# A fixed tile plan replaced by a list scheduler with a clock per engine, in a kernel of two attentions whose exponentials run on two engines

## The chip, the cores and the metric

The kernel runs on one core of a Trainium2 chip. The metric is the device time of one execution in microseconds, from the first to the last instruction of the core. Every execution is either "fast" or "slow": slow means over 1.5% above the fastest of the same kernel. Medians are over all executions of a kernel, slow ones too. Profiles are of one execution each.

Engines: TensorE (PE) multiplies, ScalarE (ACT) computes exponentials, VectorE (DVE) does elementwise work and empties PSUM, GpSimd (POOL) masks. Each has its own stream of instructions and waits at semaphores.

## The reference, cut to what matters

Two attention layers with 2048 tokens, 32 heads of 16 channels, each with its projections:

```python
# A: four segments of 512 tokens; causal softmax inside a segment, plus a memory term from earlier segments
logits = einsum('bhqd,bhkd->bhqk', qs, ks) * scale + mask
p = softmax(logits); a_dot = einsum('bhqk,bhkd->bhqd', p, vs)
...                                   # o = g * a_mem + (1 - g) * a_dot; M and z grow by phi(k) v
# B: full softmax attention over 2048 keys
p = softmax(einsum('bhqd,bhkd->bhqk', q, k) * Dh ** -0.5)
o = einsum('bhqk,bhkd->bhqd', p, v)
return concatenate([a, b], -1)        # each after its output projection
```

The work that counts is the exponentials. I call 128 keys by 512 queries of one head a *bank* (one PSUM bank). Four heads are done side by side; four banks with the same keys are a *key block*. Attention B has 512 blocks and A has 80, so there are 592 blocks or 2368 banks. A *unit* is four heads with 512 queries; B has 32 units of 16 blocks.

## The kernel before: the parts that matter

A block's exponentials are computed in one of two ways. On ScalarE: scores in PSUM tiles of three and two banks in turn, one ACTIVATE for a tile. On VectorE: four evacuations write each score, scaled and shifted, as an integer whose bits are an fp16 number (this makes a piecewise linear 2^x), and further passes add other offsets to the integers. The sum over several shifted *patterns*, each multiplied by V into the same accumulator, smooths the error. Every pattern costs four matmuls, and every pattern after the first a pass on VectorE. Lines left out below are marked; options that are switched off are dropped without a mark.

```python
LADDER = (12521, 12721, 12834, 13081, 13329)   # offsets of five patterns
PESHARE = 0.74;  VQUADS = (3, 3);  BANKS = (3, 2);  LAG = 2;  PBUFS = 6;  VBUFS = 9
# ... cut ...
def idle_work(us):            # zeros: matmuls that add nothing, to keep TensorE active
    work[0] = min(max(work[0] - us * PESHARE, -1.0), 0.25)
    acc = accs.get(cur[0])
    while acc is not None and work[0] < -0.11:
        mm(acc[:], zeros[:, 0:P], zeros[:], start=False, stop=False)
# ... cut: all tiles of ScalarE are listed beforehand; VQUADS blocks of every unit of B go to VectorE ...
def vexp(q, buf, x):          # one further pattern
    for i, off in enumerate(LADDER[1:]):
        yield 0.70
        f = vtile()
        nc.vector.tensor_scalar(f[:], x[:], float(off - LADDER[0]), 32767.0, ALU.add, ALU.min)
        vready(q, [1], f); vdone(buf)
def force():
    if pv(NT, 1): return
    if vwork and vlive[0] < VBUFS: vpiece(vwork); return
    assert step_chore()
# ... cut ...
for t in range(NT):           # one tile after the other; times only in units of tiles
    run_until(t)
    scores(t)                 # matmuls of tile t and its exponential; force() if its buffer is not free
    did = pv(t - LAG, 2)      # P x V of up to two blocks of two tiles ago
    # ... cut: one to four pieces of projections, by due tile ...
    idle_work(0.1 + 0.427 * len(tiles[t]))
    flush()
    vfill((0.08 + 0.427 * len(tiles[t])) * VSHARE - 0.69 * vscores(t))
```

## Time and profile before

| | before |
|---|---|
| time, median of four | 1014.6 us (1005.7 to 1027.6; two fast, two slow) |
| the profiled execution | 1026.1 us, slow, mean granted clock 0.955 |
| ScalarE busy / idle | 934.4 / 91.7 us |
| VectorE busy | 726.6 us |
| key blocks on VectorE | 93 (3 for each of 31 units) |

The page's table of busy time (us, share of the span, instructions), and three rows of its 40 slices; a digit is tenths, and PEclk is the clock that TensorE was granted:

```profile
PE 923.2 (90%) x7597; PEld 254.6 (25%) x7721; DVE 726.6 (71%) x1232; ACT 934.4 (91%) x828; POOL 162.2 (16%) x335
...
PE   7898989999898998989899889999989899999986
...
ACT  3799976789999999999999979999999999999984
...
PEclk8999975689999999999999999999999999999988
```

ScalarE is busiest, but in slices 6 to 9 it falls to between 6 and 8 tenths, and the clock to between 5 and 8. TensorE's row stays at 8 and 9 there. So a high busy share of TensorE is not evidence of useful speed. The Trainium skill ("Trainium Kernel Development and Optimization", Performance Expectations) calls matmul busy time a bad metric for how close a kernel is to roofline (the limit of the hardware), because matmuls are pipelined; here it also counts zeros and half-speed work.

The groups of instructions (count | busy us, mean ns of one | idle time just before them and what ended it):

```profile
L648 ACT ACTIVATE pT<-s_ps 128x1536 bf16<-128x1536 f32 (+1 forms) x799 | 923.9, 1313 | 78.1 <-PE s_ps L83 65.1
L685 DVE TENSOR_SCALAR vx<-v_ps 128x512 uint16<-128x512 f32 x372 | 254.1, 684 | 176.5 <-PE s_ps L83 117.9
L608 DVE TENSOR_SCALAR vx<-vx 128x2048 uint16<-128x2048 uint16 x372 | 243.8, 692 | 1.2
...
L83 PE MATMUL acc<-zeros 128*128 128x512 bf16 x401 | 132.4, 398 | 6.9 <-issue 6.8
```

The exponentials cost 923.9 us for (592 - 93) x 4 = 1996 banks: 0.463 us a bank, 1.85 us a block. A pattern pass over 2048 columns (692 ns) costs as much as the evacuation of a single bank of 512 (684 ns). The Trainium skill ("VectorE: DVE Perf Modes", Side-by-side: where the cycles go for N=2048 bf16) gives about 693 ns for 2048 bf16 elements in its fastest mode; these passes over 2048 16-bit integers agree.

Three stretches of the span, and after them one place closer (columns: stretch, length, busy us and count of each engine, granted clock, DMA share, GB/s):

```profile
0.00:50.00 50.00, 40.02 (x259) 13.04 (x264) 21.95 (x39) 27.04 (x25) 28.38 (x70) 0.93 0.73 148
50.00:850.00 800.00, 728.14 (x6060) 200.19 (x6158) 590.56 (x1004) 748.81 (x664) 133.78 (x265) 0.96 0.03 9
850.00:1026.10 176.10, 155.07 (x1283) 41.42 (x1299) 114.05 (x191) 158.51 (x141) 0.00 (x0) 0.95 0.02 7
```

```profile
137.00:216.00 79.00, 71.94 (x438) 14.67 (x445) 45.87 (x80) 55.80 (x49) 9.70 (x19) 0.63 0.01 2
```

ScalarE is the fourth engine column. Between 50 and 850 us it loses 51 us of 800, and 23 of these lie in the 79 us where the clock is 0.63.

### The profile page before, as it was taken

The numbers are of one execution on the slowest core, as the hardware profiler recorded it, in microseconds if no ns is written. First come the engines' busy times: TensorE is split into PE (matmuls) and PEld (weight loads), VectorE is DVE, ScalarE is ACT, GpSimd is POOL, SyncE is SP. The second block draws the span as 40 slices with busy tenths as digits, with TensorE's granted clock in tenths as the row PEclk, the third lists the DMA queues.
The fourth block names the chain that finished last, engine by engine and source line by source line (L and its number), as shares of the span: only waits on it lengthen the run. The fifth ranks groups of instructions, "written<-read, shape, count | busy, mean of one in ns | idle before, by whom it ended". The sixth has DMA issues, their size and how long they took to land.

```text
span 1026.1 us, 18868 instructions
## 1 busy us (share of the span) xinstructions
PE 923.2 (90%) x7597; PEld 254.6 (25%) x7721; DVE 726.6 (71%) x1232; ACT 934.4 (91%) x828; POOL 162.2 (16%) x335
## 2 busy tenths in 40 slices
PE   7898989999898998989899889999989899999986
PEld 2222221122222222222222222222222222222221
DVE  2657665577786888779595868868687698676762
ACT  3799976789999999999999979999999999999984
POOL 3731120030303103040200402003030300000000
PEclk8999975689999999999999999999999999999988
DMA  8500000000001000000001000000000000000000
GB/s 181 107 5 22 1 7 0 7 1 2 6 1 27 22 17 12 1 7 1 6 1 24 14 20 18 6 1 2 6 2 2 1 27 16 1 2 1 1 1 25
DMA packets 35649, 15.47 MB, mean 15 GB/s; under 512 B 27360, under 2 KB 35552, under 8 KB 35552
## 3 DMA queue, kind: packets, MB, share of 16 engines
q1 hardware_dynamic: 33776, 13.78, 5.9%
q8 instruction: 62, 1.02, 0.4%
q10 hardware_dynamic: 1776, 0.40, 0.2%
q14 instruction: 35, 0.29, 0.1%
HBM read 4.20 MB, written 4.19 MB: 8 GB/s over the span
## 4 chain that ended last, share of the span: by engine, by line
ACT 42%; PE 32%; issue 12%; DVE 9%; POOL 2%; DMA 1%; SPq 0%; ACTq 0%; DVEq 0%
ACT pT L648 41%; PE acc L83 14%; PE s_ps L83 8%; PE v_ps L83 6%; DVE vx L685 3%; PE k_ps L83 2%; PE q_ps L83 1%; DVE vx L608 1%; PE o_ps L83 1%; DVE tT L256 1%; ACT ex L197 1%; POOL pT L656 1%; DMA w_a<-in_A_wv_dram 1%; DVE qc L186 1%; SPq L159 0%
## 5 line engine op out<-in xcount | busy, mean ns | idle before, releaser
L648 ACT ACTIVATE pT<-s_ps 128x1536 bf16<-128x1536 f32 (+1 forms) x799 | 923.9, 1313 | 78.1 <-PE s_ps L83 65.1
L685 DVE TENSOR_SCALAR vx<-v_ps 128x512 uint16<-128x512 f32 x372 | 254.1, 684 | 176.5 <-PE s_ps L83 117.9
L83 PE MATMUL s_ps<-qB,KB 32*128 32x512 bf16 x1676 | 319.7, 394 | 33.3 <-ACT pT L648 24.9
L608 DVE TENSOR_SCALAR vx<-vx 128x2048 uint16<-128x2048 uint16 x372 | 243.8, 692 | 1.2
L83 PEld LDWEIGHTS <-KB 32*128 32x128 bf16 x2048 | 94.4, 91 | 322.3 <-issue 313.0
L83 PE MATMUL acc<-vx,VB 128*32 128x512 f16 x1860 | 170.4, 396 | 4.1 <-DVE vx L685 1.7
L83 PE MATMUL v_ps<-qB,KB 32*128 32x512 bf16 x372 | 146.9, 395 | 19.2 <-issue 5.6
L656 POOL TENSOR_SCALAR_AFFINE_SELECT pT<-pT 128x256 bf16<-128x256 bf16 (+2 forms) x242 | 106.1, 466 | 311.8 <-ACT pT L648 310.4
L83 PE MATMUL acc<-pT,VB 128*32 128x512 bf16 x1676 | 155.3, 398 | 0.0
L83 PE MATMUL acc<-zeros 128*128 128x512 bf16 x401 | 132.4, 398 | 6.9 <-issue 6.8
L83 PEld LDWEIGHTS <-VB 128*32 128x32 bf16 x3536 | 56.8, 95 | 141.6 <-issue 140.9
L256 DVE STREAM_TRANSPOSE tT<-acc 128x512 f32<-128x512 f32 x64 | 45.3, 708 | 30.9 <-PE acc L83 30.0
L83 PE MATMUL s_ps<-qA,kA 32*128 32x384 bf16 (+3 forms) x512 | 58.2, 305 | 9.5 <-ACT pT L648 7.1
L83 PEld LDWEIGHTS <-zeros 128*128 128x128 bf16 x480 | 38.8, 99 | 90.5 <-issue 78.3
L189 POOL TENSOR_SCALAR qA<-qc,par 128x512 bf16<-128x512 bf16 x32 | 25.8, 819 | 189.5 <-DVE qc L186 189.4
L189 POOL TENSOR_SCALAR qB<-qc,par 128x512 bf16<-128x512 bf16 x32 | 23.3, 740 | 157.9 <-DVE qc L186 157.9
L83 PE MATMUL acc<-pT,vA 128*32 128x128 bf16 (+3 forms) x512 | 34.9, 313 | 5.7 <-POOL pT L656 3.4
L186 DVE CAST qc<-q_ps 128x512 bf16<-128x512 f32 x32 | 21.9, 683 | 16.2 <-PE q_ps L83 14.6
L83 PEld LDWEIGHTS <-kA 32*128 32x128 bf16 x512 | 17.3, 92 | 50.7 <-issue 46.9
L322 DVE CAST osb<-o_ps 128x512 bf16<-128x512 f32 x28 | 19.2, 684 | 7.7 <-PE o_ps L83 7.3
L83 PE MATMUL v_ps<-w_a,xT_a 128*128 128x512 bf16 x60 | 21.1, 426 | 3.1 <-DMA w_a<-in_A_wv_dram 1.6
L83 PE MATMUL k_ps<-xT_a,w_a 128*128 128x512 bf16 x59 | 20.7, 392 | 2.2 <-DMA xT_a<-in_A_x_dram 1.1
(84 smaller groups left out, 409.7 us busy)
## 6 DMA issues: line engine op xcount, KB each, us to landing
out_dram<-osb SPq DMA_DIRECT2D x31, 128.0 KB, 1.7
w_b<-in_B_wqkv_dram SPq DMA_DIRECT2D x3, 512.0 KB, 5.7
phk<-phkT SPq DMA_TRANSPOSE x48, 2.3
w_a<-in_A_wv_dram SPq DMA_DIRECT2D x1, 512.0 KB, 7.2
wo_a<-in_A_wo_dram SPq DMA_DIRECT2D x1, 512.0 KB, 4.4
wo_b<-in_B_wo_dram SPq DMA_DIRECT2D x1, 512.0 KB, 5.2
w_a<-in_A_wk_dram SPq DMA_DIRECT2D x1, 384.0 KB, 8.8
w_a<-in_A_wq_dram SPq DMA_DIRECT2D x1, 384.0 KB, 9.4
```

The costliest lines, as they stand in the source:

```text
L83: return pin(nc.tensor.matmul(out, lhsT, rhs, **k))
L186: vlater(0.69, lambda: pin(nc.vector.tensor_copy(qc[:], ps[:])))
L189: pin(nc.gpsimd.tensor_scalar(dst[:, e, :], qc[:], par[:, e:e + 1], 0.0, ALU.mult, ALU.add))
L197: pin(nc.scalar.activation(ex[:], src, ACT.Exp))
L256: vlater(0.72, lambda: pin(nc.vector.transpose(st["tT"][:, e].rearrange("p c d -> p (c d)"), acc)))
L322: vlater(0.69, lambda: pin(nc.vector.tensor_copy(osb[:], ps[:])))
L608: pin(nc.vector.tensor_scalar(f[:], x[:], float(off - LADDER[0]), 32767.0, ALU.add, ALU.min))
L648: pin(nc.scalar.activation(pT[:, 0:n, :], pt[:, 0:n, :], ACT.Exp, scale=SCALE))
L656: pin(nc.gpsimd.affine_select(out=blk, in_=blk, compare_op=ALU.is_ge, fill=0.0, base=0, pattern=[[0, len(sls)], [1, P]], channel_multiplie ...
L685: pin(nc.vector.tensor_scalar(x[:, j, :], vt[:], XSCALE, float(LADDER[0]), ALU.mult, ALU.add))
```

## The change

The intent: no tile plan made beforehand. The program that emits the instructions keeps a clock for each engine (T) and, at each step, emits the next thing that fits before ScalarE needs its next scores. The share of VectorE is no longer a quota: a block is taken from the end of a unit's list whenever VectorE's backlog is short and PSUM has a free bank. Evacuations become tasks with ready times and priorities. Zeros are put in only when a modelled activity of the array is low and there is slack. And the ladder has four patterns, so a block costs VectorE one pass less. The diff, cut to its core:

```diff
-LADDER = (12521, 12721, 12834, 13081, 13329)
-PESHARE = 0.74
+LADDER = (12914, 13046, 13325, 13628)
-VQUADS = (3, 3)
+VMIN = 3
+VBACK = 1.2
+SWITCH = 0.095
+ACTEND = 0.166
+ACTSET = 0.081
+ACTCOL = 0.8325e-3
+WARMTH = 0.52
 ... (cut)
+    T = dict(pe=0.0, act=0.0, dve=0.0, pool=0.0)
     def mm(out, lhsT, rhs, at=0.0, **k):
+        # (cut) adds the matmul to TensorE's clock, one row or column tile beside another where they differ
+        busy.append((group["start"], group["start"] + us, 1.0 if kind == "full" else 0.25))
+    def later(us, f, src=None, prio=0, ready=None, ok=None):
+        tasks.append(dict(prio=prio, seq=seq[0], ready=ready, us=us, f=f, src=src, ok=ok))
+    def dve_run(limit):
+        # (cut) emits VectorE's tasks whose start by its clock is before limit
 ... (cut)
+        def v_scores(taken, lim=2):
+            while n < lim and backlog() < VBACK and free_slots(T["pe"] + ...) and v_pick():
 ... (cut)
-        for t in range(NT):
-            scores(t)
-            did = pv(t - LAG, 2)
-            # (cut)
-            idle_work(0.1 + 0.427 * len(tiles[t]))
+        while True:
+            dve_run(T["pe"])
+            # (cut)
+            refill(1)
+            if not stream:
+                break
+            now, rel, due = T["pe"], aend[t] + 0.06, T["act"] - HEAD   # (three lines joined)
+            if now >= rel - 0.03 and not held_back(t):
+                scores(t); t += 1
+                # (cut)
+                continue
+            slack = max(rel, due) - now + 0.05
+            # (cut) where tile t is held back by a full buffer: P x V, or a projection
+            if slack > 0.2 and step_chore(last=last):
+                continue
+            # (cut) P x V of two blocks, or of one where a buffer is needed soon
+            if slack > 0.45 and backlog() < 0.35 and v_scores(set(), 1):
+                continue
+            # (cut) more projections, P x V of one block
+            if slack > 0.2 and rel - now > 0.12 and activity(now - 2.6, now + 0.4) < WARMTH and zero():
+                continue
+            T["pe"] = min(max(now + 0.03, rel), now + 0.1)
+            # (cut)
```

In the start, the first keys are now copied by ScalarE, and the first queries are masked by VectorE instead of GpSimd.

## The prediction

> **What bounds the kernel now.** By the profile's busy table ScalarE (ACT) is busy 934 us of 1026 (91%), VectorE (DVE) 727 us (71%). The table of groups gives 923.9 us to the exponentials: 799 ACTIVATEs over 1996 banks of 512 columns, so 0.463 us a bank, 1.852 us for a key block of four banks. TensorE's 923 us is not its load: 132 us are multiplications by zeros that keep it active, and matmuls overlap. The chain of waits gives ACT 42% and TensorE 32%.
>
> By windows, ACT's 92 us of idle time fall as follows: 23 us in the first 50 (11.7 before the first exponential); about 23 at 137-216 us, where the granted clock averages 0.63; 6 at 985-1013, clock 0.76; 12 in the tail; the other 856 us lose only some 28. The profiled run is called slow; the three times, 1007 to 1028, vary, I think, with the length of such stretches at half clock. The Trainium skill ("TensorE: Matmul & The Clock Gate", Part 1) says the clock is gated to half after an idle window of TensorE; the trace agrees in size (0.50) but not plainly in cause: TensorE's busy time fell to 2.20 of 4 us only just before the stretch. It then stays there some 50 us while busy.
>
> **What the change does.**
> 1. A key block on DVE costs four evacuations (684 ns each) plus a pass of 692 ns per further pattern. Now 4 x 0.684 + 4 x 0.692 = 5.50 us, 93 blocks: 512 us, other DVE work 215 us. With four patterns instead of five: 4.81 us.
> 2. The fixed quota of three blocks per unit becomes "whenever DVE is free". The constants take a nominal 3.75 per unit, over 31 of 32 units: about 116-120 blocks. DVE then has 215 + 118 x 4.81 = 783 us. ACT keeps (592 - 118) x 1.852 = 878, plus 10 of other work: 888 us, 46 less. All of this is on the critical path, as long as ACT is the engine that doesn't wait.
> 3. P x V quads on TensorE: before 419 + 93 x 5 + 80 = 964, after 394 + 118 x 4 + 80 = 946. Nearly even.
> 4. The list scheduler should put scores ahead of ACT in the start (first keys copied by ACT, queries masked by DVE rather than GpSimd: 1-2 us) and in the mixed stages; and it inserts zeros by a modelled activity of the array, which should shorten the half-clock stretches, worth about 29 us in this trace. I expect it to get most of that, not all.
>
> **Sum.** 888 (ACT) + 20 (first 50 us) + 13 (tail) + 2% of waits in the middle (18) + about 11 for what is left of half-clock stretches = 950 us. A perfect balance of ACT and DVE would be near 134 blocks and 860 us each plus the ends, about 900, which buffers and three PSUM slots won't allow.
>
> Predicted 950 us, 8 in 10 between 926 and 985. Faster by over 2%: 0.93; within 2%: 0.05; slower: 0.02.
>
> **What would show each step.** 1: three DVE passes over 2048 columns per four evacuations, each still 690 ns. 2: evacuations at L685's successor 464-480 instead of 372; ACT's exponentials 870-890 us; DVE over 80% of the span. 4: ACT 97% or more busy between 50 us and the end; no window at granted clock 0.5 longer than 15 us; fewer than 401 zero multiplications.
>
> **What would make it wrong.** The static order relies on modelled durations; if engines in order wait for each other where the model saw none, ACT idles 5% and not 2% (+25 us). A self-sustaining half-clock stretch as at 137-216 us (+24 us each). DVE saturating with more blocks than 120 (down to 925).

## The result, and the profile after

| | before | after |
|---|---|---|
| time, median of four | 1014.6 us | 933.8 us (930.7 to 935.6, all fast) |
| ratio of fast runs | | 0.9275 (0.9243 to 0.9308) |
| ScalarE busy / idle (profiled run) | 934.4 / 91.7 us | 891.3 / 40.7 us |
| VectorE busy | 726.6 us | 759.4 us |
| key blocks on VectorE | 93 | 111 |
| zero multiplications | 401 | 508 |

A ratio here is the mean time of one kernel's fast runs over the mean of the other's fast runs of the same rounds, so it is not quite the ratio of the medians in the table. Here the fast runs are two of before, mean 1006.6 us, and all four of after, mean 933.5 us: the gain between fast runs is 73 us, where the medians differ by 81.

The same views of the changed kernel; first busy time and slices:

```profile
PE 868.7 (93%) x7609; PEld 265.6 (28%) x7609; DVE 759.4 (81%) x1265; ACT 891.3 (96%) x800; POOL 170.1 (18%) x335
...
PE   7899999999999999999999999999999999999986
...
ACT  4799999999999999999999999999999999999985
...
PEclk9799999999999999999999999999999999999998
```

ScalarE is at 9 from the third slice nearly to the end. The longest fall of the clock is near the start: in windows of 4 us it is 0.50, 0.50 and 0.72 from 24 to 36 us. A shorter one, 0.66 and 0.92 in two such windows, begins at 900 us, at the stall of experiment 7.

The groups (L774, L846 and L858 are the successors of L648, L685 and L608):

```profile
L774 ACT ACTIVATE pT<-s_ps 128x1536 bf16<-128x1536 f32 (+1 forms) x770 | 879.3, 1301 | 21.3 <-PE s_ps L104 10.8
L846 DVE TENSOR_SCALAR vx<-v_ps 128x512 uint16<-128x512 f32 x444 | 296.6, 686 | 90.5 <-PE v_ps L104 86.5
...
L858 DVE TENSOR_SCALAR vx<-vx 128x2048 uint16<-128x2048 uint16 x333 | 221.3, 708 | 1.9
...
L104 PE MATMUL acc<-zeros 128*128 128x512 bf16 x508 | 164.6, 386 | 0.0
```

444 evacuations are 111 blocks, with 333 = 3 x 111 passes. The idle time before the exponentials fell from 78.1 to 21.3 us.

The three stretches:

```profile
0.00:50.00 50.00, 40.59 (x258) 12.75 (x259) 19.75 (x35) 29.32 (x28) 28.78 (x73) 0.86 0.68 148
50.00:850.00 800.00, 761.23 (x6769) 232.83 (x6772) 678.38 (x1126) 795.89 (x715) 141.31 (x263) 1.00 0.03 9
850.00:932.00 82.00, 66.86 (x590) 20.01 (x582) 61.26 (x106) 66.09 (x60) 0.00 (x0) 0.94 0.03 9
```

Between 50 and 850 us ScalarE is now idle for 4.1 us, where it was 51. That is the largest single difference between the profiled runs; but the profiled run of before was slow, and how much of it a fast run loses has to be asked of the experiments.

The second difference is ScalarE's own work: 44.6 us less in the exponentials. 18 blocks at 1.85 us make 33 of them. The remaining 11 come from the cost of a bank: 879.3 / 1924 = 0.457 us, 0.463 before. The timeline of before shows what is cheaper, in the start, where ScalarE is starved:

```profile
11.69 1.45 ACT L648 ACTIVATE pT<-s_ps 128x1536 bf16<-128x1536 f32 x1 [8.35 <-DMA beta_t<-in_A_beta_dram]
...
15.69 1.02 ACT L648 ACTIVATE pT<-s_ps 128x1024 bf16<-128x1024 f32 x1 [2.55 <-PE s_ps L83]
...
20.03 2.37 ACT L648 ACTIVATE pT<-s_ps 128x1536 bf16<-128x1536 f32 x2 [3.31 <-PE s_ps L83]
```

A lone ACTIVATE of three banks takes 1.45 us and one of two takes 1.02, but one of each back to back takes 2.37 and not 2.47. The Trainium skill ("ScalarE: Activation LUTs", What ACT_TABLE_LOAD costs) says that back-to-back ACTIVATEs overlap by about 93 ns; the trace agrees with 0.10 us. So ScalarE, when it has to wait, is also "busy" for longer. Counted over the packed traces, there are 141 gaps between ScalarE's instructions in before and 41 after; 100 lost overlaps of 0.10 us are 10 of the 11 us. Over the runs the cost of a bank went from 0.457 us (41 gaps) to 0.477 (951.8 us for 1996 banks and 419 gaps, in the profiled run without zeros of the old order, a slow one).

### The profile page after: what moved, and what is told of

It is laid out like the page before. It is cut to its first block, busy times and chain, and to the rows that moved or that the text cites. A ratio compares the mean times of both kernels' runs of the same rounds, so it can differ in the third digit from the quotient of the medians.

```text
span 932.0 us, 18773 instructions
## 1 busy us (share of the span) xinstructions
PE 868.7 (93%) x7609; PEld 265.6 (28%) x7609; DVE 759.4 (81%) x1265; ACT 891.3 (96%) x800; POOL 170.1 (18%) x335
## 4 chain that ended last, share of the span: by engine, by line
ACT 53%; issue 24%; PE 14%; POOL 5%; DVE 3%; DMA 1%; SPq 1%; ACTq 0%; DVEq 0%; POOLq 0%
ACT pT L774 52%; PE acc L104 5%; PE s_ps L104 4%; POOL pT L784 4%; PE v_ps L104 2%; ACT ex L260 1%; PE k_ps L104 1%; POOL qB L240 1%; DMA w_a<-in_A_wv_dram 1%; PE q_ps L104 1%; DVE vx L846 1%; SPq L205 1%; DVE vx L858 0%; PE l_ps L104 0%; PE o_ps L104 0%
## 5 line engine op out<-in xcount | busy, mean ns | idle before, releaser
L774 ACT ACTIVATE pT<-s_ps 128x1536 bf16<-128x1536 f32 (+1 forms) x770 | 879.3, 1301 | 21.3 <-PE s_ps L104 10.8
L846 DVE TENSOR_SCALAR vx<-v_ps 128x512 uint16<-128x512 f32 x444 | 296.6, 686 | 90.5 <-PE v_ps L104 86.5
L104 PE MATMUL s_ps<-qB,KB 32*128 32x512 bf16 x1604 | 253.9, 383 | 28.3 <-ACT pT L774 22.1
L858 DVE TENSOR_SCALAR vx<-vx 128x2048 uint16<-128x2048 uint16 x333 | 221.3, 708 | 1.9
L104 PE MATMUL acc<-zeros 128*128 128x512 bf16 x508 | 164.6, 386 | 0.0
L104 PE MATMUL v_ps<-qB,KB 32*128 32x512 bf16 x444 | 157.0, 384 | 0.5 <-DVE vx L846 0.2
L104 PEld LDWEIGHTS <-KB 32*128 32x128 bf16 x2048 | 85.7, 91 | 243.5 <-issue 235.8
L104 PEld LDWEIGHTS <-VB 128*32 128x32 bf16 x3380 | 71.6, 94 | 150.3 <-issue 140.1
L104 PEld LDWEIGHTS <-zeros 128*128 128x128 bf16 x524 | 40.7, 98 | 96.0 <-issue 86.1
L104 PE MATMUL s_ps<-qA,kA 32*128 32x512 bf16 (+3 forms) x512 | 53.5, 306 | 8.3 <-ACT pT L774 4.9
L238 DVE CAST qc<-q_ps 128x512 bf16<-128x512 f32 x31 | 21.3, 686 | 8.7 <-PE q_ps L104 8.1
L280 DVE CAST VB<-v_ps 128x512 bf16<-128x512 f32 x16 | 11.0, 690 | 12.6 <-PE v_ps L104 12.6
```

The costliest lines, as they stand in the source:

```text
L104: return pin(nc.tensor.matmul(out, lhsT, rhs, **k))
L238: pin(nc.vector.tensor_copy(qc[:], ps[:]))
L280: pin(nc.vector.tensor_copy(dst, ps[:].rearrange("p (h d) -> p h d", d=DH)))
L774: pin(nc.scalar.activation(pT[:, 0:n, :], pt[:, 0:n, :], ACT.Exp, scale=SCALE))
L846: pin(nc.vector.tensor_scalar(x[:, j, :], vt[:], XSCALE, float(LADDER[0]), ALU.mult, ALU.add))
L858: pin(nc.vector.tensor_scalar(p[:], x[:], float(off - LADDER[0]), 32767.0, ALU.add, ALU.min))
```

## The experiments

Twelve kernels, three rounds each unless said. Their runs of before, 29 with the four above, lie between 1005.7 and 1027.7 us, but for one of 1051.4 and one of 1179.8.

The mean granted clock of each run helps with every comparison below. The 18 fast runs of before in these jobs lie within 1.4 us of a straight line, from 1006.1 us at clock 0.983 to 1022.6 at 0.961: some 7.2 us for each 0.01 of clock. So their spread goes with the clock. Where I say "at the same clock" below, I mean the distance from this line (worked out after all runs; beyond 0.983 it is extended).

The theory: ScalarE is the bound. Moving blocks is worth ScalarE's time for them, patterns are worth nothing but the blocks that they make room for, and the order is worth the idle time of ScalarE.

### 1. Four patterns in the old order

```diff
 # before
-LADDER = (12521, 12721, 12834, 13081, 13329)
+LADDER = (12914, 13046, 13325, 13628)
```

> The old order and its fixed quota of three blocks, with four patterns for five (93 vector passes of 0.69 us, 64 us of VectorE time, taken away). Theory: ScalarE is the bound and keeps its 1996 banks, so the time stays within 1% of before (ratio 0.99 to 1.01). Rival A (the vector passes themselves, or the 372 matmuls fewer, held the kernel up): ratio below 0.98.

Measured: 1014.1 us, ratio 1.001 (0.989 to 1.014).

```profile
PE 911.2 (90%) x7313; PEld 256.4 (25%) x7438; DVE 673.2 (66%) x1139; ACT 932.1 (92%) x828; POOL 162.7 (16%) x335
...
L83 PE MATMUL acc<-zeros 128*128 128x512 bf16 x475 | 155.8, 392 | 6.6 <-issue 6.1
```

VectorE's busy time fell from 726.6 to 673.2 us and the time did not measurably move. Rival A falls, as its 0.98 lies outside: VectorE's passes were not what bounds the kernel. The edit did one thing more than I meant: `idle_work` filled the place of the missing matmuls, and the zeros rose from 401 to 475. At the same clock the four runs are 4 to 5 us faster than before, so the patterns may be worth a little by themselves, with a lower clock hiding it. This profiled run was fast, so it also shows what a fast run of the old order loses: ScalarE was busy 932.1 of 1012.5 us, idle 80. So of the 92 idle us of the slow run most are there in a fast one too.

### 2. Four patterns and 108 blocks in the old order

```diff
 # before, with the ladder of experiment 1
-VQUADS = (3, 3)
+VQUADS = (4, 3)
```

> The old order with four patterns and a quota of 4 and 3 in turn: 108 blocks on VectorE where the change has 111. Theory: the 15 blocks moved are worth 15 x 1.85 = 28 us of ScalarE, and the old order keeps its idle time of about 70 us in a fast run: ratio about 0.972. Rival B (the share alone makes the gain): ratio about 0.94 or lower. Rival C (the old fixed order cannot use more blocks, new waits eat the gain): ratio above 0.99.

Measured: 1023.4 us, ratio 1.017 (1.006 to 1.028). The theory's number is a miss, and rival B is far off; rival C (above 0.99) is what came. By the rule of 2% the verdict is unclear, but the whole interval lies above 1.

```profile
PE 905.1 (89%) x7420; PEld 254.5 (25%) x7539; DVE 733.4 (72%) x1244; ACT 907.9 (89%) x804; POOL 158.6 (16%) x333
```

ScalarE's busy time did fall, from 932.1 us in experiment 1 to 907.9 (24 us, where 28 were worked out), but its idle time rose from 80 to 113. Part of what ate the gain can be seen in the timeline of this run, here ScalarE, VectorE and TensorE around the longest such place:

```profile
343.48 1.45 ACT L648 ACTIVATE pT<-s_ps 128x1536 bf16<-128x1536 f32 x1 [0.25 <-PE s_ps L83]
...
345.20 4.90 DVE L608 TENSOR_SCALAR vx<-vx 128x2048 uint16<-128x2048 uint16 x8
345.94 4.01 PE L83 MATMUL acc<-vx,VB 128*32 128x512 f16 x28 [1.38 <-DVE vx L608]
350.15 0.62 PE L83 MATMUL acc<-vx,VB 128*32 128x512 f16 x8 [0.20 <-DVE vx L608]
...
350.92 0.39 PE L83 MATMUL s_ps<-qB,KB 32*128 32x512 bf16 x2
...
351.41 1.02 ACT L648 ACTIVATE pT<-s_ps 128x1024 bf16<-128x1024 f32 x1 [6.48 <-PE s_ps L83]
```

36 matmuls of patterns stand in TensorE's order ahead of the next scores, four at a time behind VectorE's passes and at their pace (eight in 4.90 us), and ScalarE waits 6.48 us for the scores behind them. The Trainium skill ("TensorE: Matmul & The Clock Gate", Part 2, Step-by-step) says that matmuls stay in program order; this stretch agrees. The code's `force()` makes such lumps, when a buffer has to come free; that it was this call here is inferred from the code. In all, TensorE waited 10.8 us at accumulations for a pattern pass (23 times), 1.3 us in before. In the old order more share is no gain, and at the same clock a loss of some 8 us against experiment 1: the order was what stood in the way of the share.

### 3. The new order with at most three blocks per unit, five patterns and four

```diff
 # after
-                if u["name"] == "a" or len(u["kbs"]) < VMIN:
+                if u["name"] == "a" or len(u["kbs"]) < VMIN or u.get("nv", 0) >= 3:
 # and, in the run with five patterns only, the old LADDER
```

> The new list scheduler with five patterns and at most three blocks per unit: 91 blocks on VectorE, so order alone. Theory: ScalarE's busy time stays near before's (two blocks more, +4 us) and its idle time falls to about 40 us: about 969 us, ratio about 0.963. Rival B: ratio near 1.00.

> The new scheduler with four patterns, at most three blocks per unit: 92 blocks. Theory: 933.8 + 19 x 1.83 = 969 us, the same as the run with five patterns within 5 us, because patterns cost only VectorE time. Rival A: clearly faster (over 10 us) than the run with five patterns.

Measured: with five patterns (91 blocks) 973.1 us, ratio 0.963 (0.956 to 0.970), where 969 and 0.963 were expected; with four (92 blocks) 965.4 us, ratio 0.958 (0.951 to 0.964). The profiled run with five patterns:

```profile
PE 889.4 (91%) x7719; PEld 282.7 (29%) x7839; DVE 723.9 (74%) x1216; ACT 928.1 (95%) x832; POOL 161.6 (17%) x334
```

So the order alone (with its new rule for zeros and the new start), with two blocks fewer than before on VectorE and the same patterns, gives 41 us on the medians, some 37 by the ratio of fast runs, and 33 to 34 at the same clock: one of its runs had 975.3 us at 0.979, one of before 1009.6 at 0.979. ScalarE is idle for 45 us, where the fast run of experiment 1 had 80. Rival B falls. So most of what the order gives does not come from a better clock.

The two runs differ by 8 us, and I had allowed 5: a small miss. The profiles show a part of it. ScalarE's busy time is 928.1 and 924.0 us, and with five patterns ScalarE lost 3.5 us in a stretch (175 to 200 us, clock 0.80) where with four it lost 0.6 (clock 1.00). The rest is open.

### 4. The new order with five patterns, share left free

```diff
 # after
-LADDER = (12914, 13046, 13325, 13628)
+LADDER = (12521, 12721, 12834, 13081, 13329)
```

> The changed kernel with the five old patterns; the scheduler may still give VectorE whatever it has time for, and then gives 101 blocks (111 with four patterns). Theory: the fourth pattern's omission is worth the 10 blocks, 10 x 1.83 = 18 us, plus the few us seen between the two runs with three blocks per unit (8 us): 952 to 960 us, ratio to before 0.945 to 0.952. Rival (the share is set elsewhere, by buffers or PSUM, and patterns do not matter): within 5 us of 933.8.

Measured: 948.8 us, ratio 0.934 (0.923 to 0.946); the range expected was 952 to 960, so the patterns were worth a little less than worked out, 15 us on the medians and not 18 or more. The rival (within 5 us of 933.8) falls. Taking the three together on the new side: the free share with five patterns gains 24 us over the limited one (973.1 to 948.8, ten blocks more; that is above the 18 that ten blocks are worth; the half-clock stretch just named may be part of it), and the fourth pattern's omission 15 us more (ten blocks more).

### 5. Zeros: none in the new order, more and none in the old

```diff
 # after, "no zeros"
-WARMTH = 0.52
+WARMTH = 0.0
 # before, "more zeros" and "no zeros"
-PESHARE = 0.74
+PESHARE = 0.85        # and 0.0
```

> The changed kernel without any of the zero multiplications that the scheduler adds when its modelled activity of the array is low (109 blocks on VectorE, so +4 us from the share). Theory: half-clock stretches come back, mean granted clock below 0.95, ScalarE starved in them: 960 us or more. Rival (real work is dense enough now, zeros do nothing): 934 to 942 us and a clock of 0.98.

> The kernel before with more zero multiplications (its target share of TensorE 0.85 for 0.74), nothing else. Theory: of the 37 to 40 us that order alone gained, most is the half-clock stretches of the old order, so with them gone the old order comes near: mean clock 0.98 or more and a ratio of 0.97 to 0.985. Rival (the half clock is a by-product; the old order starves ScalarE by its order, and more zeros only stand in the way of scores): ratio 1.00 or above.

> The kernel before without zero multiplications (the other end of the run with more zeros). The changed kernel lost 41 us without its zeros, at a clock of 0.876. Theory: the old order loses at least as much, clock below 0.9, ratio 1.04 or more. Rival: the old order's zeros hinder as much as they help, ratio within 1% of 1.

| order | zero multiplications | mean clock of the profiled run | median us | ratio to before |
|---|---|---|---|---|
| old | 0 | 0.673 (slow run) | 1174.6 (three of four slow; the fast one 1141.8, clock 0.713) | none given |
| old | 401 (as it is) | 0.955 (slow run) | 1014.6 | 1 |
| old | 770 | 0.993 | 1045.4 | 1.031 (1.019 to 1.044) |
| new | 0 | 0.876 | 974.9 | 0.959 (0.947 to 0.971) |
| new | 508 (as it is) | 0.987 | 933.8 | 0.9275 |

(The ratios are each to the runs of before in the same job.) The new order without zeros loses 41 us, as the theory said. The old order without zeros loses some 130 (its fast run against the fast ones of before in that job, 1012.3 us on average). One execution of before itself, 1179.8 us, lies beside its slow ones: it has no profile, but the record gives its mean clock as 0.64, so with all its zeros it too ran at a low clock most of the time. Why is not known.

The run with more zeros shows my theory wrong in one point. I took the half-clock stretches for most of the old order's idle time and expected that more zeros would win it back. They did raise the clock to 0.993, and the kernel was 3% slower, 45 to 47 us slower at the same clock: the rival came. Here are the lines of that run: busy time, zeros, and the middle stretch.

```profile
PE 970.3 (93%) x7977; PEld 263.6 (25%) x8115; DVE 727.4 (70%) x1232; ACT 949.1 (91%) x828; POOL 161.7 (16%) x335
```

```profile
L83 PE MATMUL acc<-zeros 128*128 128x512 bf16 x770 | 239.0, 384 | 9.7 <-issue 9.1
```

```profile
50.00:850.00 800.00, 751.48 (x6247) 204.81 (x6353) 580.06 (x988) 746.74 (x654) 132.98 (x265) 1.00 0.03 8
```

At a mean clock of 1.00 in this stretch, ScalarE is still idle for 53 of 800 us, as much as in before's slow run (51) and more than in the fast run of experiment 1 (44). And its exponentials are dearer, 936.8 us for 923.9, as it pauses 261 times and not 141. The edit adds nothing but zeros, so they cause the loss. Counted in the traces, zeros stand in TensorE's order between the scores of the tile before and those waited for in 145 of 239 waits of ScalarE, and in 39 of 132 in before. These 145 waits are 35 of 80 us; how the zeros bring about the others was not traced.

So the clock and the order are one problem: TensorE has to be kept active *in the gaps that ScalarE leaves*, and the old loop, which knows only an average share per tile, cannot tell a gap from a place where scores are due. (How much of the order's gain lies in this is not shown.) The new order places 508 zeros, more than before, and ScalarE is idle for 4.1 of 800 us. Their number is not what matters: with five patterns and a free share (experiment 4) it placed 395, fewer than before and beside more matmuls of patterns, at a clock of 0.989. (The old rule counts a row tile as half a matmul and a column tile as 0.3, the new one both as a quarter; this too may matter and was not tried alone.)

### 6. A wrong clock

```diff
 # after
-ACTCOL = 0.8325e-3
+ACTCOL = 0.9158e-3
```

> The changed kernel with one wrong constant: the scheduler takes ScalarE's time per column 10% too long. It then gives VectorE 121 blocks and plans 971 us. Theory (the modelled durations matter, as TensorE gets more between two score tiles than ScalarE leaves time for): ScalarE waits for scores all along, 945 us or more although its own work falls by 18 us. Rival (engines in order correct the plan by themselves): 905 to 925 us.

Measured: 947.0 us, ratio 0.938 (0.933 to 0.944), in the range that the theory expected. ScalarE's waits for TensorE in the two runs, first the changed kernel and then the one with the wrong constant (total us, times, longest):

```profile
ACT pT L774 <- PE s_ps L104: 10.8, 11, 3.3
...
ACT pT L774 <- PE v_ps L104: 5.5, 6, 3.2
```

```profile
ACT pT L774 <- PE s_ps L104: 22.4, 43, 3.4
ACT pT L774 <- PE v_ps L104: 11.3, 27, 3.4
```

With ten blocks fewer on ScalarE (worth 18 us) the kernel is 13 us slower, so the error of 10% costs some 31 us. The profiles account for most: ScalarE is idle for 59.3 us and not 40.7, and busy for 883.4, only 8 less instead of 18, as it pauses 140 times and not 41. The scheduler also put in 632 zeros for 508. The rival is half right too: the plan said 971 us, and the engines, each in order, ran it in 947. The durations matter, but an error is not paid in full.

### 7. The checks of the sums as tasks

In the trace after, the last unit holds one long stall, and it comes from work that the scheduler emits without counting it: the check that the softmax sums are in range.

```profile
897.39 0.69 DVE L397 TENSOR_REDUCE okm<-okt 128x1 f32<-128x512 bf16 x1
...
899.86 1.89 DVE L858 TENSOR_SCALAR vx<-vx 128x2048 uint16<-128x2048 uint16 x3
900.60 0.40 PE L104 MATMUL acc<-vx,VB 128*32 128x512 f16 x4 [3.82 <-DVE vx L858]
...
901.42 1.02 ACT L774 ACTIVATE pT<-s_ps 128x1024 bf16<-128x1024 f32 x1 [3.21 <-PE v_ps L104]
```

VectorE does the checks, the pattern pass comes after them, TensorE waits 3.82 us for it and ScalarE 3.21 us for the scores behind.

```diff
 # after, in unit_done
-                    fin_half(wk, st, e)
+                    later(0.7, lambda: fin_half(wk, st, e), ready=T["dve"])
                     if e == 0:
-                        sums_ok(wk, 0, 32, okm[:, 0:1], "a")
-                        sums_ok(wk, 32, 63, okm[:, 1:2], "b")
+                        later(1.9, lambda: sums_ok(wk, 0, 32, okm[:, 0:1], "a"), prio=3, ready=T["dve"])
+                        later(1.9, lambda: sums_ok(wk, 32, 63, okm[:, 1:2], "b"), prio=3, ready=T["dve"])
```

> The changed kernel with the six passes of the check of the sums (some 4 us of VectorE, which the scheduler did not count and put into the middle of the last unit, where TensorE then waited 3.8 us for a pattern and ScalarE 3.2 us) handed to the scheduler as tasks of the lowest priority. Theory: that stall goes; one block fewer on VectorE (110): 1 to 4 us faster than the changed kernel, ratio to before about 0.925. Rival (slack elsewhere swallows it): no difference within 1 us.

Measured: 928.8 us (927.9 to 930.7), ratio 0.915 (0.905 to 0.926); the changed kernel had 930.7 to 935.6, so this is 5 us on the medians, with one block less on VectorE. In its trace ScalarE runs its exponentials without a pause for 30.9 us from 883.9 on, so the stall is gone. The 5 us are a little more than expected, the two kernels did not run in the same rounds, and the schedule changed elsewhere too (428 zeros for 508), so not all of the difference need be the stall.

### 8. More share, and three patterns (five rounds each)

```diff
 # experiment 7
-VBACK = 1.2
+VBACK = 1.6
-            if slack > 0.45 and backlog() < 0.35 and v_scores(set(), 1):
+            if slack > 0.45 and backlog() < 1.3 and v_scores(set(), 1):
 # and, in the second run only
-LADDER = (12914, 13046, 13325, 13628)
+LADDER = (13338, 13617, 14003)
-VNOM = 3.75
+VNOM = 4.0
```

> The run with the checks as tasks, with the scheduler's two limits on VectorE's queue loosened (blocks may be started with a backlog of up to 1.6 us, 1.2 before, and alone with up to 1.3 us, 0.35 before): 118 blocks instead of 110. Theory (ScalarE is still the bound): 8 x 1.83 = 15 us less, given that PSUM and order hold: 914 to 920 us. Rival (VectorE's evacuations of q, k, v and outputs now come late, and ScalarE waits): 925 us or more.

> As the run with more share, and three fp16 patterns (13338, 13617, 14003; worked out to have a ripple of 0.24% rms where the four have 0.17% and the five 0.12%): a block costs VectorE 4 x 0.69 + 2 x 0.70 = 4.2 us, and the scheduler gives it 130 blocks. Theory: 12 more blocks than the run with more share, 22 us less: 892 to 900 us, and correct. Rival: waits eat it, above 905 us; or the result is no longer correct.

Measured: with 118 blocks and four patterns 918.1 us (916.7 to 919.0), ratio 0.9075 (0.904 to 0.911); with 130 blocks and three patterns 893.3 us (891.4 to 894.6), ratio 0.883 (0.880 to 0.886), and correct. Both lie in the theory's ranges. The lines of the run with three patterns:

```profile
PE 847.5 (95%) x7263; PEld 255.4 (29%) x7263; DVE 748.6 (84%) x1268; ACT 855.5 (96%) x769; POOL 163.0 (18%) x333
...
L774 ACT ACTIVATE pT<-s_ps 128x1536 bf16<-128x1536 f32 x739 | 844.2, 1307 | 18.6 <-PE s_ps L104 16.0
```

ScalarE is still the bound at 96%, and the waits before its exponentials (18.6 us, 21.3 in the changed kernel) have not grown. This version beats both kernels, by 4% and by 12%. Its result passed the same comparison with the reference; how near it came to the limit of that comparison was not measured. The offsets were chosen by arithmetic: the ripple of the sum of three is worked out as 0.24% rms, of the four in the change 0.17%, of the five 0.12%.

## Why the prediction was right, and where it was not

The measured 933.8 us lies in the range of 926 to 985, 16 us under the 950 predicted.

- **"ScalarE is the engine that doesn't wait; patterns and share count through it."** Right. Four patterns alone gave nothing (ratio 1.001), and the kernels of the new order, but for the two with zeros or clock spoilt, went by their blocks: 965.4 us with 92, 948.8 with 101, 933.8 with 111, 918.1 with 118, 893.3 with 130, which is (965.4 - 893.3) / 38 = 1.9 us a block, where 1.85 was predicted. The steps between are uneven (1.7 from 92 to 111, 2.1 from 118 to 130), the runs of 118 and 130 have experiment 7 in them, worth 5 us with one block less, and the limited run with five patterns lies apart (973.1 with 91, against 965.4 with 92).
- **"About 116-120 blocks ... ACT keeps 878, plus 10."** 111 blocks and 891.3 us (444 evacuations, where 464 to 480 were to show the step). Two errors that cancelled: seven blocks fewer than 118 should have cost 13 us, and the cheaper bank (0.457 for 0.463 us, because ScalarE no longer pauses) gave back 11. I had taken a constant named as nominal (3.75 a unit) for the outcome (3.6).
- **"Other DVE work 215 us."** 759.4 - 296.6 - 221.3 = 241.5 us. I had multiplied mean durations by counts, which counts overlaps twice; busy times (254.1 + 243.8 = 497.9 us) leave 228.7 in before. VectorE's 81%, near the 783 of 950 us worked out (82%), came out of these two errors in opposite directions: more other work, fewer blocks.
- **The sum's last terms: "2% of waits in the middle (18) + about 11 for what is left of half-clock stretches".** This is the mis-sized step. Between 50 and 850 us ScalarE was idle for 4.1 us in all, so the 29 us allowed came to about 8 with the stall of the last unit (3.2 + 0.9 us). The ends were right: 20.7 us of idle in the first 50 (20 predicted), 15.9 us after 850, of which 4.1 is that stall (13 predicted for the tail). 891.3 + 20.7 + 4.1 + 15.9 = 932.0.
- **"The list scheduler ... should shorten the half-clock stretches."** Right, but worth less than reckoned: the longest left is some 10 us at the start (24 to 36 us). "About 29 us in this trace" was read from a slow run at clock 0.955. Fast runs of before, at up to 0.983, lie some 20 us below it, and the new order is 33 to 34 us faster at the same clock (experiment 3). So most of its gain is not a better clock. **"Fewer than 401 zero multiplications"** is wrong: there are 508. I thought that a better order would need fewer; it made room for more. It does need zeros (41 us lost without any, experiment 5), but 395 sufficed with five patterns.
- **What the prediction left out:** that order and share do not add up. It reckoned the share as 46 us "as long as ACT is the engine that doesn't wait", and nearly the same share in the old order, 108 blocks, gained nothing (experiment 2). The order is not a second gain beside the share but its condition.
- **"A perfect balance ... about 900, which buffers and three PSUM slots won't allow."** Not tested as it stands, as it was meant for four patterns: with four patterns and right constants the most tried was 118 blocks, 918.1 us. With three patterns the same buffers and slots took 130 blocks and gave 893.3 us.

What stays open: what exactly lowers the clock; how the 33 to 41 us of the order divide among the placement of zeros, of projections and of pattern matmuls, the new rule for zeros and the new start (idle time in the first 50 us: 23.0 before, 20.7 after); and a few us between five and four patterns at a limited share.

## What to carry to other kernels

Move work to an engine that isn't the bound only together with an order that can use it: here 108 blocks gained nothing in a fixed order, and 111 saved time in one that reckons when each engine is due. What stands ahead of the critical instruction in an engine's order can delay it, filler too (36 pattern matmuls, 6.48 us; 369 more zeros, 3%), so put filler into gaps and not in by an average. Compare runs at the same clock where it varies. A scheduler depends on its durations (10% in one constant cost some 31 us), so count every instruction that it emits, the rare checks at the end included.

## What the Trainium skill lacked or had wrong

- "TensorE: Matmul & The Clock Gate", Part 1 (What's actually happening): the clock is halved after at least one idle window of about 3.4 us, and full again after about 3.4 us of sustained work. That fits the stall of experiment 7: TensorE waited 3.82 us, and the clock was 0.66 and 0.92 in the two windows of 4 us from 900 us. But in the fast run of experiment 1 TensorE had no such gap (its longest wait in the 12 us before, from 300 to 312, was 1.00 us), and then stayed at 0.50 for some 36 us while its busy row read 3.5 to 4 of 4 us:

```profile
308.00:312.00 4.00, 2.91 (x29) 1.07 (x25) 3.54 (x7) 3.67 (x3) 4.00 (x9) 0.96 0.00 0
312.00:316.00 4.00, 3.64 (x28) 0.92 (x28) 2.40 (x7) 2.48 (x2) 0.73 (x3) 0.50 0.10 33
316.00:320.00 4.00, 4.00 (x26) 0.61 (x24) 1.59 (x5) 2.36 (x2) 0.00 (x0) 0.50 0.01 4
...
344.00:348.00 4.00, 4.00 (x17) 0.65 (x17) 1.98 (x3) 1.64 (x3) 0.00 (x0) 0.50 0.07 25
348.00:352.00 4.00, 3.96 (x29) 0.84 (x21) 2.45 (x5) 3.38 (x3) 0.00 (x0) 0.85 0.02 4
```

- The same page, further on in Part 1, does report cases that its rule of one window leaves out: a kernel whose clock swings because TensorE micro-idles often between groups of matmuls, and a gate seen stuck low for over 50 us. What it lacks is how to tell from a profile which case a stretch like the one above is; no run here shows it either.
- In that stretch, at least, the busy time of the profile was not what released the clock: 0.50 at 4.00 busy of 4. The matmuls here are mostly tiles of 32 rows or 32 columns; the changed kernel counts each as a quarter of a full matmul, and with that rule had a mean clock of 0.987. That such tiles count for less is not shown alone by any run, and I found no statement of it on that page.
- The same page's practical advice is to avoid gaps. It doesn't say that multiplications by zeros can keep up the clock of a kernel that has too little other work, nor what they cost: with 0, 401 and 770 of them the profiled runs of the old order had mean clocks of 0.673, 0.955 (both slow runs) and 0.993, and the medians were 1174.6, 1014.6 and 1045.4 us.
- "ScalarE: Activation LUTs" has the overlap of back-to-back ACTIVATEs right (0.10 us here). It could add what follows for reading a profile: the busy time of ScalarE is inflated where it waits, here from 0.457 us a bank with 41 gaps to 0.477 with 419.
